# Sliding-window attention and a gated MLP in parallel: P times V of two pairs of head groups in one run

## Chip, cores and metric

The kernel runs on one core of a Trainium2 chip. The metric is the device time of one execution in microseconds, the median of several runs. The profile is one execution, taken by the hardware profiler; its times count from the first instruction.

## The reference

A layernorm without weights feeds two branches, which are added to the input: attention with 32 heads of 20 over a causal window of 256, and a gated MLP with a sigmoid gate. All inputs are bf16; x is 1 x 2048 x 640.

```python
xn = _layernorm(x)                                   # over D = 640
q, k, v = split_heads(xn @ wqkv)                     # 32 heads of 20
scores = (q @ k.T) * 20 ** -0.5                      # per head
mask = (i - j >= 0) & (i - j < 256)
o = softmax(where(mask, scores, -1e9)) @ v
A = o @ wo
B = (sigmoid(xn @ w_gate) * (xn @ w_up)) @ w_down    # F = 1536
return x + A + B
```

## The kernel before

The rows are worked on in four chunks `c` of 512. For each chunk there are these kinds of work for TensorE (PE):

- `qk`: ten projection blocks (`proj_block`, L297), five for Q and five for K, of five matmuls of 512 columns each. Q blocks are copied out of PSUM by VectorE (DVE, L301), K blocks by ScalarE (ACT, L303). The copies go by DMA into a DRAM scratch and come back in the layout that the scores need (`spread`, L315).
- `v`: eight half blocks (L326), two per 128 rows, five matmuls of 320 columns each; DVE copies out the first half, ACT the second.
- `gu`: twelve pairs of blocks `pg` and `pu` (L411, L418). ACT takes tanh of `pg`, DVE makes `h` from that and `pu` (L422).
- `out`: for each 128 rows the down projection (L432) and the attention output projection (L439) into the same two accumulators, then the residual (L443, DVE) and the store.
- scores: heads are in eight groups of four. Two groups, a pair `o` of 0, 2, 4 or 6, are worked on together, in four score steps in chunk 0 (`FIRST`) and five in the later ones (`LATER`). A step is 16 or 24 small matmuls (L487) on 20 x 64 tiles of the array, into one PSUM tile `ps` of four banks with one buffer. ACT takes the exponential of the whole tile into `pT` in SBUF (L493). Then the parts on the diagonal and on the window's old edge are masked: by GpSimd (POOL) with `affine_select` (L504), or, in the `late` steps, by DVE with a minimum against the tile `edge` (L497).
- P times V: `pv` (L520) multiplies all `pT` tiles of a pair with V, 72 matmuls in chunk 0 and 96 later, into two PSUM accumulators. `finish_group` turns each accumulator into `t1` with a DVE transpose (L532), and `scale_group` divides by the row sums and gathers the heads for the output projection (L540, L544, L548, all DVE).

All accumulators but `ps` come from the pool `ps_d` of four PSUM banks; each block needs one, a P times V two.

The order of work is written out by hand. The main loop (L719 on) goes over 76 score steps (16 in chunk 0, 20 in each later one). Around them an object `Fill` gives out the other PE work, the fill, from a list of labelled parts (L689 to L707). `fill.pull(ns)` takes blocks until their costs (1080 for a block, 680 for half a V block, and so on) add up to `ns`; `fill.until(label)` takes all up to that part. A part whose label is in `fill.shut` stops the pulling. After each score step at least `APART` = 1800 is pulled, and more by a credit, so that all the fill ahead of the next `out` part is spread over the steps up to a cut:

```python
credit += fill.left(label) / (last - t)
```

Work that is put off (`scale_group`) waits in `fill.behind`; each pulled block lets one of them go, or two where `hurry` is set. `due` says ahead of which step a pair's `pv` comes: one step after the pair's last score step, two in chunk 0. So before, the order is fill, `pv`, scores, fill, sixteen times less the last pair, which is worked on at the end.

Loads and stores are issued by SyncE (SP), in order; layernorm tiles are turned by DMA transposes on the same queue (`turn_block`, L283).

Of the kernel before, what the change touches and what calls it, by code (L numbers as in the profile page):

```python
# [9 lines left out]
P = 128  # L10
S = 2048
D = 640
# [3 lines left out]
DC = D // P  # L16
FC = F // P
CW = 512
NCH = S // CW
SBC = CW // P  # L20
HG = 4
NG = H // HG
GH = NG // 2
# [22 lines left out]
U = 64  # L46
PTW = 10 * U

# [14 lines left out]
FIRST = (  # L63
    dict(pieces=((0, 0, 5, 0), (5, 5, 3, 5)), diag=(0, 2), old=(4, 1), units=8),
    dict(pieces=((1, 1, 5, 0), (6, 6, 2, 5), (4, 7, 1, 7)), diag=(0, 2), old=(4, 1), units=8),
    dict(pieces=((2, 2, 5, 0), (7, 7, 1, 5)), diag=(0, 2), old=(4, 1), units=6),
    dict(pieces=((3, 3, 5, 0), (4, 4, 3, 5)), diag=(0, 2), old=(4, 1), units=8),
)
LATER = (
    dict(pieces=((2, 2, 5, 2), (-3, 0, 2, 0), (7, 7, 1, 7)), diag=(2, 2), old=(1, 2), units=8),  # L70
    dict(pieces=((3, 3, 5, 1), (6, 6, 2, 6), (-4, 0, 1, 0)), diag=(1, 2), old=(0, 2), units=8),
    dict(pieces=((0, 0, 5, 3), (-2, 0, 3, 0)), diag=(3, 1), old=(2, 2), units=8),
    dict(pieces=((1, 1, 5, 0), (5, 5, 3, 5)), diag=(0, 2), old=(4, 1), units=8),
    dict(pieces=((-1, 0, 4, 0), (4, 4, 4, 4)), late=3, units=8),
)
# [18 lines left out]
def kernel(  # L94
# [22 lines left out]
    xtp = pool("xtp", 2)  # L117
    stp = pool("stp", 6)
    qp = pool("qp", 3)
    kp = pool("kp", 5)  # L120
    vp = pool("vp", 10)
    hp = pool("hp", 15)
    pp = pool("pp", 5)
    op = pool("op", 7)
    onp = pool("onp", 2)
    tp = pool("tp", 2)
    np_ = pool("np", 2)
    ps_d = pool("ps_d", 4, space=bass.MemoryType.PSUM)
# [106 lines left out]

    edge = const.tile([P, HG, 2 * U], BF16, name="edge")

    def make_edge():
        nc.gpsimd.memset(edge, BIG)
        for k, base, sign in ((0, -1, -1), (1, 0, 1)):  # L240
            for a in range(2):
                view = edge[a * U:(a + 1) * U, :, k * U:(k + 1) * U]
                nc.gpsimd.affine_select(out=view, in_=view, pattern=[[0, HG], [sign, U]],
                                        compare_op=GE, fill=0.0, base=base, channel_multiplier=-sign)

    xnT = {}
    xns = {}

# [21 lines left out]
    def norm_block(c, s, mv, rstd):  # L270
        xn = lnp.tile([P, D], BF16, name="xn")
        nc.vector.tensor_scalar(out=xn, in0=xc[c][:, s, :], scalar1=mv[:, 0:1],  # L272
                                scalar2=rstd[:, 0:1], op0=SUB, op1=MULT)
        xns[c, s] = xn

    def transpose_rows(s, copy, lo=0, hi=DC):
        pt = ps_h.tile([P, DC, P], BF16, name="pt", tag="h")
        for d in range(lo, hi):
            nc.tensor.transpose(pt[:, d, :], xns[0, s][:, d * P:(d + 1) * P], ident)  # L279
        copy(out=xnT[0][:, lo:hi, s * P:(s + 1) * P], in_=pt[:, lo:hi, :])  # L280

    def turn_block(c, s):
        nc.sync.dma_start(out=xnT[c][:, :, s * P:(s + 1) * P], in_=xns.pop((c, s)), transpose=True)  # L283

# [81 lines left out]
    def g_qk(c):  # L366
        for w in "qk":
            for m in range(DC):
                proj_block(w, c, m)
                if c == 0 and w == "q" and m == 1:  # L370
                    load_x(1)
                if c == 0 and w == "q" and m == 3:
                    load_gu(wu, B_w_up, 0, FS // 2)
                if c == 1 and w == "q" and m == 3:
                    load_wo()
                if c and w == "k" and m == DC - 1:
                    spread("q", c, 0, GH)
                yield 5 * MM
        if c == 0:
            spread("q", c, 0, 2)  # L380
            spread("k", c, 0, 2)
            spread("q", c, 2, 4)
            spread("k", c, 2, 4)

    def g_v(c):
        for s in range(SBC):
            new_v(c, s)
            for hf in range(2):
                proj_v(c, s, hf, nc.scalar.copy if hf else nc.vector.tensor_copy)
                if hf == 0:  # L390
                    yield 5 * 136
            if s == 0:
                spread("k", c, 0, 2)
                spread("k", c, 2, GH)
            if s == 1:
                spread("q", c, GH, NG)
                spread("k", c, GH, NG)
            yield 5 * 136
# [81 lines left out]
    def scores(c, o, step):  # L480
# [12 lines left out]
        nc.scalar.activation(out=pt[:, :, 0:width], in_=ps[:, :, 0:width], func=EXP, scale=SCALE)  # L493
        if "late" in step:
            u = step["late"]
            view = pt[:, :, u * U:(u + 2) * U]
            return pt, lambda: nc.vector.tensor_tensor(out=view, in0=view, in1=edge, op=MIN)  # L497

        for (u, n), base, sign in ((step["diag"], 0, 1), (step["old"], -1, -1)):
            for a in range(2):  # L500
                two = pt[a * U:(a + 1) * U].rearrange("p h (a b) -> p h a b", a=2)
                k, b = divmod(u, SPAN)
                view = two[:, :, k:k + n, b * U:(b + 1) * U]
                nc.gpsimd.affine_select(out=view, in_=view, pattern=[[0, HG], [0, n], [sign, U]],  # L504
                                        compare_op=GE, fill=0.0, base=base, channel_multiplier=-sign)
        return pt, None

# [19 lines left out]

    on = {}

    def finish_group(c, g, acc):  # L530
        t1 = np_.tile([P, 16, 32], FP32, name="t1")
        nc.vector.transpose(out=t1.rearrange("p b r -> p (b r)"), in_=acc)  # L532
        if c < NCH - 1 or g < NG - 2:
            fill.behind.append(lambda: scale_group(c, g, t1))
        else:
            scale_group(c, g, t1)

    def scale_group(c, g, t1):
        rec = np_.tile([P, 16, 1], FP32, name="rec")
        nc.vector.reciprocal(rec, t1[:, :, DH:VW])  # L540
# [73 lines left out]
    def mean_act(s):  # L614
        xn = lnp.tile([P, D], BF16, name="xn")
        neg = lnp.tile([P, 1], FP32, name="neg")
# [8 lines left out]

    def norm_act(s, xn, neg, r):
        nc.vector.reciprocal(r, r)
        nc.vector.tensor_scalar(out=xn, in0=xc[0][:, s, :], scalar1=neg[:, 0:1],  # L628
                                scalar2=r[:, 0:1], op0=ADD, op1=MULT)
        xns[0, s] = xn  # L630

# [10 lines left out]
    for lo, hi in ((0, 3), (3, DC)):  # L642
        transpose_rows(0, act, lo, hi)
    norm_act(1, xn1, neg1, r1)
    mv3 = ln_mv(ln_half(0, 3, 1, stats3))
# [9 lines left out]
    v01 = project_v(0, 0, 1)  # L655
    norm_act(2, xn2, neg2, r2)
    copy_v(0, 0, 0, v00, act, (1,))
# [37 lines left out]
    fill.add("qk1", g_qk(1), 50 * MM)  # L695
    fill.add("v1", mix(g_v(1), g_gu(1, 0, 2), 1, 2), 40 * 136 + 2 * GU)
    fill.add("out0", mix(g_out(0, g_gu(1, 2, 3)), norms2, 1, 1), OUT + GU)
    fill.add("x3", later(load_x, 3), 0)
    fill.add("qk2", g_qk(2), 50 * MM)
    fill.add("v2", mix(g_v(2), g_gu(1, 3, 7), 0, 1), 40 * 136 + 4 * GU)  # L700
    fill.add("gu1b", mix(g_gu(1, 7, 12), norms3, 0, 1, False), 5 * GU)
    fill.add("out1", mix(g_out(1, g_gu(2, 0, 1)), itertools.chain(norms3, g_turns(3)), 1, 2), OUT + GU)
    fill.add("qk3", g_qk(3), 50 * MM)
    fill.add("v3", mix(g_v(3), g_gu(2, 1, 5), 0, 1), 40 * 136 + 4 * GU)
    fill.add("gu2", g_gu(2, 5, 12), 7 * GU)
    fill.add("out2", g_out(2, (), g_gu(3, 0, 1)), OUT + GU)
# [5 lines left out]

    due = {t + (1 if n else 2): (n, o) for (n, o), t in ends.items()}
    cuts = [(ends[n, NG - 2] + 2 + n, f"out{n}") for n in range(NCH - 1)] + [(len(todo), None)]
    fill.pull(6 * 5 * MM)
    parts = {}
    credit = 0
    fill.shut = {"out0", "out1", "out2"}
    for t, (c, k, o, step) in enumerate(todo):  # L719
        if k == 0 and c > 0:  # L720
            fill.until(f"qk{c}")
        if k == 2 and c > 0:
            fill.until(f"v{c}")
        if t in due:
            fill.flush()
            pair = due[t]
            fill.hurry = pair[1] == NG - 2
            pv(*pair, parts.pop(pair))
            if pair[1] == NG - 2:
                fill.shut.discard(f"out{pair[0]}")  # L730
        pt, late = scores(c, o, step)
        parts.setdefault((c, o), []).append((step, pt))
        last, label = next(x for x in cuts if t < x[0])
        credit += fill.left(label) / (last - t)
        rest = APART
        if late:
# [12 lines left out]

    homes = [("rows", 3)] * (SBC - 1) + [("xn", 4)]  # L750
    rows = [new_rows(c, s, *home, queue=nc.scalar) for s, home in enumerate(homes)]
    banks.close()
# [54 lines left out]
```

## Time and profile before

| | |
|---|---|
| time, median of 3 runs | 309.05 us (308.9 to 309.46) |
| profiled execution: span from first to last instruction | 307.5 us |
| the profiled execution's own time | not given beside its span; the median lies 1.55 us above the span |
| PE busy | 299.6 us, 97% |
| DVE, ACT, POOL busy | 170.7, 198.4, 169.3 us |
| scores (L487), P times V (L520) on PE | 1440 matmuls each; 8.7% and 6.0% of the chain of waits |
| `affine_select` on POOL (L504) | 256, 157.7 us |
| masks on DVE (L497) | 12, 5.1 us |
| granted TensorE clock | 1.000 |

Busy times are those of one engine; engines work beside each other. "Idle before" names what ended a wait. In the timeline a line gives the start, the time that the merged instructions took, the engine, the source line, and the tiles. The chain of waits follows the execution back from its last instruction, at each step to what released it.

### The profile page before, as it was taken

To read this page: it belongs to the slowest core of one execution; us is meant where nothing else is said; L and a number is where in the kernel's file an instruction comes from. 1 tells how busy PE (TensorE), PEld (TensorE's weight loads), DVE (VectorE), ACT (ScalarE), POOL (GpSimd) and SP (SyncE) were. 2 spreads that over 40 slices of the span, in tenths; PEclk is the share of its full clock that TensorE was granted. 3 is DMA by queue.
4 is the path that set the end of the run, shared out by engine and by line. 5 is a ranking of instruction groups with operands and counts; after the bars stand their busy time and mean duration, and the time that the engine had idled before them with its cause. 6 is when DMAs were issued, how large, how long until landed. Compare 5 with 4: busy or idle time off the path is not lost.

```text
span 307.5 us, 9944 instructions
## 1 busy us (share of the span) xinstructions
PE 299.6 (97%) x4276; PEld 167.5 (54%) x4311; DVE 170.7 (56%) x339; ACT 198.4 (65%) x197; POOL 169.3 (55%) x308
## 2 busy tenths in 40 slices
PE   7999999999999999999999999999999999999995
PEld 3654444555657654554457654554546664444774
DVE  5633666639698364487946164392824536363523
ACT  6933877698855649888674547878585547687000
POOL 6000686787874828576683729467372937566000
PEclk9999999999999999999999999999999999999999
DMA  7997976986407352820002712730000200000202
GB/s 215 366 344 236 324 158 214 337 238 209 154 2 139 58 179 68 272 83 2 3 3 67 129 58 87 250 122 0 5 0 2 87 26 21 2 2 7 83 21 67
DMA packets 40460, 35.68 MB, mean 116 GB/s; under 512 B 10560, under 2 KB 39872, under 8 KB 40384
## 3 DMA queue, kind: packets, MB, share of 16 engines
q1 hardware_dynamic: 39552, 34.27, 37.3%
q10 hardware_dynamic: 864, 0.77, 0.9%
q8 instruction: 34, 0.56, 0.8%
q14 instruction: 10, 0.08, 0.1%
HBM read 23.63 MB, written 10.26 MB: 110 GB/s over the span
## 4 chain that ended last, share of the span: by engine, by line
PE 96%; issue 1%; DMA 1%; DVE 1%; ACT 0%; SPq 0%
PE y L432 18%; PE pu L418 17%; PE pg L411 17%; PE pqk L297 14%; PE ps L487 9%; PE pv L326 7%; PE y L439 7%; PE acc L520 6%; DMA xc<-in_A_x_dram 1%; PE pt L279 0%; ACT xn L617 0%; DVE xn L272 0%; DVE xn L628 0%; SPq L156 0%; DVE stats L252 0%
## 5 line engine op out<-in xcount | busy, mean ns | idle before, releaser
L504 POOL TENSOR_SCALAR_AFFINE_SELECT pT<-pT 64x512 bf16<-64x512 bf16 (+1 forms) x256 | 157.7, 616 | 108.1 <-ACT pT L493 95.6
L493 ACT ACTIVATE pT<-ps 128x2048 bf16<-128x2048 f32 (+1 forms) x76 | 141.0, 1855 | 59.6 <-PE ps L487 54.6
L422 DVE SCALAR_TENSOR_TENSOR h<-th,pu 128x512 bf16<-128x512 f32 x48 | 32.8, 684 | 52.6 <-PE pu L418 46.1
L418 PE MATMUL pu<-xnT,wu 128*128 128x512 bf16 x228 | 59.0, 380 | 0.7 <-issue 0.2
L411 PE MATMUL pg<-xnT,wg 128*128 128x512 bf16 x226 | 58.5, 380 | 0.9 <-issue 0.3
L432 PE MATMUL y<-wd,h 128*128 128x320 bf16 (+2 forms) x396 | 56.7, 295 | 0.0
L432 PEld LDWEIGHTS <-h 128*128 128x128 bf16 x396 | 36.7, 98 | 15.8 <-issue 2.0
L414 ACT ACTIVATE th<-pg 128x512 f32<-128x512 f32 x48 | 28.6, 595 | 15.5 <-PE pg L411 15.4
L411 PEld LDWEIGHTS <-wg 128*128 128x128 bf16 x240 | 22.2, 98 | 25.8 <-issue 1.8
L418 PEld LDWEIGHTS <-wu 128*128 128x128 bf16 x240 | 22.0, 98 | 25.5 <-issue 2.0
L487 PE MATMUL ps<-qT,kT 20*64 20x320 bf16 (+4 forms) x1440 | 32.1, 260 | 0.0
L532 DVE STREAM_TRANSPOSE t<-acc 128x512 f32<-128x512 f32 x32 | 21.1, 697 | 19.7 <-PE acc L520 19.7
L487 PEld LDWEIGHTS <-kT 20*64 20x64 bf16 x1440 | 15.4, 103 | 24.9 <-issue 21.8
L443 DVE SCALAR_TENSOR_TENSOR rows<-y,rows 128x320 bf16<-128x320 f32 x30 | 14.4, 488 | 25.5 <-PE y L439 25.3
L544 DVE TENSOR_TENSOR on<-t,rec 128x320 bf16<-128x320 f32 (+4 forms) x48 | 27.8, 580 | 1.1
L326 PE MATMUL pv<-wv,xnT 128*128 128x320 bf16 x160 | 25.7, 300 | 0.0
L439 PE MATMUL y<-wo,oc 128*128 128x320 bf16 (+2 forms) x165 | 24.2, 295 | 0.0
L297 PE MATMUL pqk<-xnT,wk 128*128 128x512 bf16 x97 | 23.1, 381 | 0.2
L297 PE MATMUL pqk<-xnT,wq 128*128 128x512 bf16 x94 | 22.8, 381 | 0.4 <-issue 0.2
L335 DVE CAST v<-pv 64x320 bf16<-64x320 f32 x29 | 14.1, 486 | 12.5 <-PE pv L326 12.3
L520 PE MATMUL acc<-pT,v 64*32 64x320 bf16 (+4 forms) x1440 | 19.7, 253 | 0.0
L520 PEld LDWEIGHTS <-v 64*32 64x32 bf16 x1440 | 16.2, 91 | 5.8 <-ACT pT L493 1.7
(50 smaller groups left out, 178.7 us busy)
## 6 DMA issues: line engine op xcount, KB each, us to landing
qT<-sq SPq DMA_DIRECT2D x16, 256.0 KB
kT<-sk SPq DMA_DIRECT2D x16, 256.0 KB
sq<-st SPq DMA_DIRECT2D x20, 128.0 KB
sk<-st SPq DMA_DIRECT2D x20, 128.0 KB
out_dram<-rows SPq DMA_DIRECT2D x15, 160.0 KB
wg<-in_B_w_gate_dram SPq DMA_DIRECT2D x4, 480.0 KB
wu<-in_B_w_up_dram SPq DMA_DIRECT2D x4, 480.0 KB
xc<-in_A_x_dram SPq DMA_DIRECT2D x3, 640.0 KB
```

Of the source, the lines that this page charges most:

```text
L297: nc.tensor.matmul(ps, lhsT=wt[:, m, :], rhs=xnT[c][:, d, :], start=(d == 0), stop=(d == DC - 1))
L326: nc.tensor.matmul(ps[:, 0:HALF], lhsT=xnT[c][:, d, s * P:(s + 1) * P], rhs=wqkv[2][:, d, hf * HALF:(hf + 1) * HALF], start=(d == 0), stop ...
L411: nc.tensor.matmul(pg, lhsT=part(wg, d, f), rhs=xnT[c][:, d, :], start=(d == 0), stop=(d == DC - 1))
L414: nc.scalar.activation(out=th, in_=pg, func=TANH, scale=0.5)
L418: nc.tensor.matmul(pu, lhsT=part(wu, d, f), rhs=xnT[c][:, d, :], start=(d == 0), stop=(d == DC - 1))
L422: nc.vector.scalar_tensor_tensor(out=h, in0=th, scalar=1.0, in1=pu, op0=ADD, op1=MULT)
L432: nc.tensor.matmul(y[:, 0:cut[1] - cut[0]], lhsT=ht[c, f][:, s * P:(s + 1) * P], rhs=wd[:, f, cut[0]:cut[1]], start=(f == 0), stop=False)
L439: nc.tensor.matmul(y[:, 0:cut[1] - cut[0]], lhsT=oc[c, m][:, s * P:(s + 1) * P], rhs=wo[:, m, cut[0]:cut[1]], start=False, stop=(m == DC - 1))
L487: nc.tensor.matmul(ps[a * U:(a + 1) * U, i, col * U:(col + n) * U], lhsT=qk["k", kc, o // GH][32 * i:32 * i + DH, o % GH + a, kb * U:(kb + ...
L493: nc.scalar.activation(out=pt[:, :, 0:width], in_=ps[:, :, 0:width], func=EXP, scale=SCALE)
L504: nc.gpsimd.affine_select(out=view, in_=view, pattern=[[0, HG], [0, n], [sign, U]], compare_op=GE, fill=0.0, base=base, channel_multiplier ...
L520: nc.tensor.matmul(acc[32 * i:32 * i + 32, q * U:(q + n) * U], lhsT=vt[kb][a * U:(a + 1) * U, u, h * VW:h * VW + 32], rhs=pt[a * U:(a + 1) ...
```

## The change

P times V of two pairs now comes in one run, after the scores of its step instead of before, and no fill is pulled in that step. Chunks 0 to 2 have two such runs each, chunk 3 one, and then one single pair as before. To hold the probabilities of two pairs, `pT` has 11 buffers of 8 units (512) instead of 5 of 10. The pairs of masks in the step tables are split: two neighbouring units (an old edge and a diagonal) are masked by DVE in one minimum, in all steps of chunk 0 and three of five later; POOL masks the rest one unit at a time. `edge` holds one head's mask and is broadcast over four. There are fewer Q, K, V, `st` and `oc` tiles; the normalised rows are written in place, so the load of the next rows waits for their turning. V of each chunk is split into two parts; the second (`v1b`, `v2b`, `v3b`) is shut until the last P times V of the chunk before. The spreads of Q and K move from the projection parts into the main loop. With three `t1` tiles, the fourth accumulator of a run waits for the scaling of the first.

```diff
-PTW = 10 * U
+PTW = 8 * U
 FIRST = (
-    dict(pieces=((0, 0, 5, 0), (5, 5, 3, 5)), diag=(0, 2), old=(4, 1), units=8),
+    dict(pieces=((0, 0, 5, 0), (5, 5, 3, 5)), diag=(0,), pair=4, units=8),
...
 LATER = (
-    dict(pieces=((2, 2, 5, 2), (-3, 0, 2, 0), (7, 7, 1, 7)), diag=(2, 2), old=(1, 2), units=8),
-    dict(pieces=((3, 3, 5, 1), (6, 6, 2, 6), (-4, 0, 1, 0)), diag=(1, 2), old=(0, 2), units=8),
-    dict(pieces=((0, 0, 5, 3), (-2, 0, 3, 0)), diag=(3, 1), old=(2, 2), units=8),
-    dict(pieces=((1, 1, 5, 0), (5, 5, 3, 5)), diag=(0, 2), old=(4, 1), units=8),
-    dict(pieces=((-1, 0, 4, 0), (4, 4, 4, 4)), late=3, units=8),
+    dict(pieces=((2, 2, 5, 2), (-3, 0, 2, 0), (7, 7, 1, 7)), diag=(2,), old=(1,), pair=6, units=8),
+    dict(pieces=((3, 3, 5, 1), (6, 6, 2, 6), (-4, 0, 1, 0)), diag=(1,), old=(0,), pair=5, units=8),
+    dict(pieces=((0, 0, 5, 3), (-2, 0, 3, 0)), diag=(3,), old=(2, 7), units=8),
+    dict(pieces=((1, 1, 5, 0), (5, 5, 3, 5)), diag=(0, 5), old=(4,), units=8),
+    dict(pieces=((-1, 0, 4, 0), (4, 4, 4, 4)), pair=3, units=8),
 )
-    stp = pool("stp", 6)
-    qp = pool("qp", 3)
-    kp = pool("kp", 5)
-    vp = pool("vp", 10)
+    stp = pool("stp", 5)
+    qp = pool("qp", 2)
+    kp = pool("kp", 4)
+    vp = pool("vp", 8)
-    pp = pool("pp", 5)
-    op = pool("op", 7)
+    pp = pool("pp", 11)
+    op = pool("op", 6)
-    np_ = pool("np", 2)
+    np_ = pool("np", 3)
...
-        xn = lnp.tile([P, D], BF16, name="xn")
-        nc.vector.tensor_scalar(out=xn, in0=xc[c][:, s, :], scalar1=mv[:, 0:1],
+        xn = xc[c][:, s, :]
+        nc.vector.tensor_scalar(out=xn, in0=xn, scalar1=mv[:, 0:1],
...
     def finish_group(c, g, acc):
+        if len(turned) == 3:
+            fill.behind.pop(0)()
...
-    fill.add("v1", mix(g_v(1), g_gu(1, 0, 2), 1, 2), 40 * 136 + 2 * GU)
+    fill.add("v1", mix(g_v(1, 0, 2), g_gu(1, 0, 1), 1, 2), 20 * 136 + GU)
+    fill.add("v1b", mix(g_v(1, 2, 4), g_gu(1, 1, 2), 1, 2), 20 * 136 + GU)
...
-    fill.add("v2", mix(g_v(2), g_gu(1, 3, 7), 0, 1), 40 * 136 + 4 * GU)
-    fill.add("gu1b", mix(g_gu(1, 7, 12), norms3, 0, 1, False), 5 * GU)
+    fill.add("v2", mix(g_v(2, 0, 2), g_gu(1, 3, 5), 0, 1), 20 * 136 + 2 * GU)
+    fill.add("gu1b", mix(g_gu(1, 5, 12), norms3, 4, 1, False), 7 * GU)
+    fill.add("v2b", g_v(2, 2, 4), 20 * 136)
...
-    due = {t + (1 if n else 2): (n, o) for (n, o), t in ends.items()}
-    cuts = [(ends[n, NG - 2] + 2 + n, f"out{n}") for n in range(NCH - 1)] + [(len(todo), None)]
+    due = {}
+    for n in range(NCH):
+        wait = 1 if n else 2
+        for o in (0, 4):
+            if n == NCH - 1 and o == 4:
+                due[ends[n, o] + wait] = [(n, o)]
+            else:
+                due[ends[n, o + 2] + wait] = [(n, o), (n, o + 2)]
+    cuts = [(ends[n, NG - 2] + 3, f"out{n}") for n in range(NCH - 1)] + [(len(todo), None)]
-    fill.shut = {"out0", "out1", "out2"}
+    fill.shut = {"out0", "out1", "out2", "v1b", "v2b", "v3b"}
...
+    def products(pairs):
+        fill.flush()
+        if pairs[0][0]:
+            fill.until("v%db" % pairs[0][0])
+        last = pairs[-1][1] == NG - 2
+        fill.hurry = last
+        for pair in pairs:
+            pv(*pair, parts.pop(pair))
+        if last:
+            fill.shut -= {f"out{pairs[0][0]}", f"v{pairs[0][0] + 1}b"}
...
+        if k == 1 and c > 0:
+            spread("q", c, GH, NG)
+            spread("k", c, GH, NG)
+        if o >= GH and f"qk{c + 1}" in fill.done:
+            spread_first(c + 1)
+        pairs = due.get(t, ())
+        if len(pairs) == 1:
+            products(pairs)
         pt, late = scores(c, o, step)
         parts.setdefault((c, o), []).append((step, pt))
         last, label = next(x for x in cuts if t < x[0])
         credit += fill.left(label) / (last - t)
+        if len(pairs) == 2:
+            products(pairs)
+            if late:
+                late()
+            continue
```

`spread_first(c)` issues the first halves of Q and K of a chunk once, in two pieces each. The third chunk's V is split like the second's, with `gu2` ahead of `v3b`. The rows of the last chunk's residual are loaded into the tile of x instead of three `rows` tiles and one `xn`.

## Prediction

> **What bounds the kernel now.** I read the engine shares and the chain of waits first, then the timeline of PE, ACT and DVE around the P times V runs, then the groups by shape.
>
> ```profile
> PE 299.6 (97%) x4276; PEld 167.5 (54%) x4311; DVE 170.7 (56%) x339; ACT 198.4 (65%) x197; POOL 169.3 (55%) x308
> ...
> PE 96%; issue 1%; DMA 1%; DVE 1%; ACT 0%; SPq 0%
> ```
>
> TensorE is never kept waiting: 96% of the chain is its own work. A gain has to shorten its work, and any wait that a change gives it is added to the end. So the two questions are what PE time the change removes and whether PE ever waits.
>
> ```profile
> 28.01 1.24 PE L411 MATMUL pg<-xnT,wg 128*128 128x512 bf16 x5
> 29.09 1.24 PE L418 MATMUL pu<-xnT,wu 128*128 128x512 bf16 x5
> 30.26 0.42 PE L487 MATMUL ps<-qT,kT 20*64 20x320 bf16 x16
> ...
> 93.72 1.52 PE L439 MATMUL y<-wo,oc 128*128 128x320 bf16 x10
> 95.17 1.29 PE L520 MATMUL acc<-pT,v 64*32 64x320 bf16 x96
> 96.39 0.43 PE L487 MATMUL ps<-qT,kT 20*64 20x320 bf16 x24
> 96.75 2.62 PE L432 MATMUL y<-wd,h 128*128 128x320 bf16 x18
> ```
>
> Start to start: a fill block of five takes 1.08 (28.01 to 29.09), but 1.17 when a score step follows (29.09 to 30.26), so fill to small tiles costs 0.09. A P times V of 96 takes 1.22; it streams 40 units of 64 columns, 1.08 at the block's 1.08/2560 columns, so leaving it costs 0.14. A score step takes 0.36 and streams 512 columns, 0.22: another 0.14 to leave.
>
> ```profile
> 72.72 0.60 ACT L414 ACTIVATE th<-pg 128x512 f32<-128x512 f32 x1
> 73.22 1.44 ACT L493 ACTIVATE pT<-ps 128x1536 bf16<-128x1536 f32 x1
> 74.69 0.85 ACT L335 CAST v<-pv 64x320 bf16<-64x320 f32 x2
> 75.64 1.88 ACT L493 ACTIVATE pT<-ps 128x2048 bf16<-128x2048 f32 x1
> ```
>
> The score matmuls of the last line start at 75.06, so EXP starts 0.58 behind them and lasts 1.88. The score tile has one buffer: the next score step can't start sooner than 2.5 us after the last, however little lies between. Today two fill blocks (2.6 with the step) cover that.
>
> ```profile
> 146.66 1.31 DVE L532 STREAM_TRANSPOSE t<-acc 128x512 f32<-128x512 f32 x2
> 148.27 0.69 DVE L422 SCALAR_TENSOR_TENSOR h<-th,pu 128x512 bf16<-128x512 f32 x1 [0.30 <-PE pu L418]
> 148.88 0.25 DVE L540 RECIPROCAL rec<-t 128x16 f32<-128x16 f32 x1
> 149.16 0.75 DVE L544 TENSOR_TENSOR on<-t,rec 128x128 bf16<-128x128 f32 x1
> 149.94 0.71 DVE L548 STREAM_TRANSPOSE oc<-on 128x512 bf16<-128x512 bf16 x1
> 150.58 0.32 DVE L544 TENSOR_TENSOR on<-t,rec 128x192 bf16<-128x192 f32 x1
> 150.81 0.24 DVE L540 RECIPROCAL rec<-t 128x16 f32<-128x16 f32 x1
> 151.09 0.67 DVE L544 TENSOR_TENSOR on<-t,rec 128x320 bf16<-128x320 f32 x1
> 151.79 0.71 DVE L548 STREAM_TRANSPOSE oc<-on 128x512 bf16<-128x512 bf16 x1
> ```
>
> One P times V leaves DVE 1.3 of transposes and 3.55 (148.88 to 152.43) of scaling. It comes every fifth step, and DVE catches up between. These numbers price the merge.
>
> **The change, part by part.** *Merged runs.* Seven pairs are merged (two each in chunks 0, 1, 2, one in 3). Two separate runs pay fill to P 0.09, P to scores 0.14, scores to fill 0.14, twice: 0.74. Merged, the order is fill, S, P, P, S, fill: 0.09 + S to P + 0.14 + 0.14, with no switch between the P's. No row shows S to P; the nearest is scores to fill, 0.14, which I take: 0.23 saved, 7 x 0.23 = 1.6 us. With S to P at nothing it is 2.6, at twice 0.14 it is 0.6. [...]
>
> *The score steps around a merged run get no fill.* In chunks 1 to 3, S and two P take 0.36 + 1.08 + 1.22 = 2.66, over EXP's 2.5: nothing lost. In chunk 0 a P (72) takes 0.97, so 0.36 + 0.81 + 0.97 = 2.14: 0.4 lost at steps 9 and 17 each.
>
> *Fill runs dry at steps 15 to 17.* I walked the pacing by the kernel's own costs (1080 a block, 680 half a V block, at least 1800 per step). For the kernel before, the walk gives the trace's order of blocks. For the new one: `left("out0")` counts v1b (4880), but v1b stays shut until the merged run of step 17, so the open work is spent early. Step 14 gets pg, v, v; step 15 one block; step 16 none; step 17 the merged run. PE then waits on EXP. ACT is also late, with EXP and two copies per step (1.88 + 0.6 + 0.6 = 3.1, against 2.6 of PE) in steps 11 and 12 and 1.88 + 0.6 + 0.85 in step 13, so EXP of 15 starts 0.8 late. Step 14 waits 0.2, step 16 1.9 (S 0.36 and one block 1.08 in an interval of 3.3), step 17 2.15 (2.5 less 0.36), step 18 0.3: 4.5 us. Without the lag 3.8, with a longer one 5.
>
> *DVE after a merged run.* It now has four transposes (2.6), four groups to scale (7.0) and the masks, and each fill block that DVE empties queues behind them, with four PSUM banks in all. Step 36, from its score start: transposes at 1.7 to 3.65, scaling (2.2) to 5.85 because only three t1 fit, fourth transpose 6.5, mask 6.9, h of pu 7.6, two groups 10.6, mask 11.0, last group 12.7, h of the next pu 13.4, V copies (0.99 each) 14.4 and 15.4. PE from 3.0: three gate/up blocks to 6.2, V halves from 6.5; at 9.0 pu, v220 and v230 hold three banks for DVE, and the fourth passes two tiles through ACT; the second down tile waits for 13.4. PE ends these nine pieces at 15.1, where its work alone ends at 12.2: 3 us. Step 56 queues the same: 3 us. Step 17 has V at once and four layernorm blocks on DVE (1.0 each): PE reaches step 19 at 15.7, by its work 13.6: 2.1 us. Step 9 (Q copies on DVE) 0.5. Steps 26, 46 and 66 have ACT-emptied or gate/up blocks between: 0.3 together. Bounds: with DVE's products as short as its quickest rows (0.25 to 0.5, POOL quiet) 1, 1 and 0.7; if banks come round in strict turn, step 36 waits for h at 13.4 and for the V copies after it: 5.6 each.
>
> [...]
>
> *Masks.*
>
> ```profile
> L504 POOL TENSOR_SCALAR_AFFINE_SELECT pT<-pT 64x512 bf16<-64x512 bf16 x176 | 120.8, 686 | 101.8 <-ACT pT L493 93.9
> L504 POOL TENSOR_SCALAR_AFFINE_SELECT pT<-pT 64x256 bf16<-64x256 bf16 x80 | 37.0, 462 | 6.3 <-ACT pT L493 1.7
> L497 DVE TENSOR_TENSOR pT<-pT,edge 128x512 bf16<-128x512 bf16 x12 | 5.1, 425 | 8.0 <-ACT pT L493 7.9
> ```
>
> POOL goes from 256 selects to 272 narrow ones: 272 x 0.462 = 126 us for 157.7. DVE goes from 12 to 52 masks: 17 us more, and each waits for its EXP with the next evacuation behind it (7.9 over 7 waits, 1.1 each). With one block of two behind it and a bank to spare this is hidden; uncovered it is counted above.
>
> *SP and buffers, at nothing.* Spreads move from steps 12 to 15 (chunk 1) to steps 14 and 17. Queued ahead is the last K store; score step 16, 6 us on, waits for it. Cover: SP's waits for K stores are 2.1 over 5 in all. Uncovered: 1 us. load_x now waits for the turns, which are four steps older; behind it on SP are wo_i, wd and pads, due much later. Q, K, V, st and oc tiles fall free before their new use in the walk; the in-place norm has the same instruction.
>
> **Sum.** -1.6 + 0.4 (step 9) + 4.5 + 2.1 + 3 + 3 + 0.5 + 0.3 = +12.2 us, with 17's 0.3 in the 4.5. The profile gives a span of 307.5 and no other own time; the median 309.05 lies 1.55 above, taken as unchanged. Span 319.7, time 321.2.
>
> **The rivals.** *Banks cover the burst.* DVE's products run at their quick rows, and steps 36, 56, 17 give 1 + 1 + 0.7, the rest nothing: -1.6 + 0.4 + 4.5 + 2.7 = +6: 315. For: the trace has DVE four layernorm blocks behind at 87 to 91 with PE busy. Against: nine pieces, four banks.
>
> *The clock falls in the dry spell.* The granted clock is 1.00 in every window, the last included, where PE does 0.93 of 4.5 us; that speaks against it. The ten warm-up matmuls took 3.99 (0.40 each, later 0.216). If a spell sends PE back to that for 4 us, it costs 1.85; one to three spells: 323 to 327. [...]
>
> *Faster: the switch is worth more.* Place: the seven merged runs. All that a P times V pays beyond streaming is 0.09 + 0.14 + 0.14 = 0.37, so 2.6 at most. It decides only where all waits sum to less: it needs v1 to last through step 16 and the bursts hidden. Then 309.05 - 1.6 = 307.4. Against: the walk fits the trace.
>
> *The change does nothing*, both sides cancelling: needs 1.6 of waits, and step 16 alone has 1.9.
>
> **How the numbers follow.** Forecast 0.68 (316 to 326), covered burst 0.16, clock 0.11, faster 0.03, nothing 0.02. Time 321.2. Lower bounds (-2.6 + 0.4 + 3.8 + 2.7) give 313.4, upper ones (-0.6 + 0.8 + 5 + 3 + 5.6 + 5.6 + 1) 329.5; the range 313.4 to 327 leaves out the fast cases and the far end. Within 0.2% (0.6 us, what a measurement tells apart): 0.02; slower 0.95.
>
> **What would show it.** PE busy share of the span down to 93 to 94%; a PE gap of some 2 us before each of two neighbouring score steps ahead of the chunk 1 runs, released by ACT's pT; gaps before V or y released by DVE after the second merged run of chunks 1 and 2; P times V pairs of 2.3 start to start; POOL near 130 us, DVE near 188. Wrong if scores of step 16 have fill ahead, if PE stays at 97%, or if the gaps name a DMA.

## The result, and the profile after

The changed kernel takes 331.15 us (median of four, 328.71 to 336.62) beside 309.04 for the kernel before on the same chip: a ratio of 1.069, 95% interval 1.065 to 1.073. Runs over 1.5% above the fastest of their kernel are left out of the ratios: one of these four (336.62), and three of the four of x3_phase below. By the medians it is 22.1 us slower, where 12.2 was forecast, and 4 us above the range. The profiled execution has a span of 329.6; its own time, 331.34, is 1.7 above the span.

The engine shares, the clock row, the row of one DMA queue and the chain of the changed kernel:

```profile
PE 306.9 (93%) x4278; PEld 170.9 (52%) x4311; DVE 175.6 (53%) x379; ACT 198.9 (60%) x197; POOL 130.1 (39%) x324
...
PEclk9999999979799997999899999999999999999999
...
q8 instruction: 34, 0.56, 0.7%
...
PE 82%; DMA 6%; DVE 4%; issue 4%; ACT 3%; SPq 0%; ACTq 0%; DVEq 0%
```

PE's share is 93%, as forecast, but it gets there in two ways. Its idle time between instructions grew from 3.5 to 18.9 us, and its busy time from 299.6 to 306.9 although it does the same matmuls. The clock row tells why the second: it falls below 9 in four places. The trace has four stretches there, from 70.24, 83.89, 124.85 and 162.40, each 3.41 us long, at a granted clock of 0.50. In the chain there is now 4% of "issue", time in which PE waited for nothing that the profile shows.

The PE timeline at the dry spell of steps 16 and 17:

```profile
80.23 0.43 PE L479 MATMUL ps<-qT,kT 20*64 20x320 bf16 x24 [1.30 <-ACT pT L485]
82.76 0.43 PE L479 MATMUL ps<-qT,kT 20*64 20x320 bf16 x24 [2.10 <-ACT pT L485]
83.12 2.18 PE L510 MATMUL acc<-pT,v 64*32 64x320 bf16 x120
```

These are the two waits that were forecast, 1.30 and 2.10 for 1.9 and 2.15. Then the timeline behind the runs of steps 26 and 36, in the run of step 46, and at step 56:

```profile
119.28 2.39 PE L510 MATMUL acc<-pT,v 64*32 64x320 bf16 x192
121.60 0.33 PE L479 MATMUL ps<-qT,kT 20*64 20x320 bf16 x3
123.68 0.42 PE L479 MATMUL ps<-qT,kT 20*64 20x320 bf16 x21 [1.75 <-issue]
124.03 3.72 PE L297 MATMUL pqk<-xnT,wq 128*128 128x512 bf16 x9
...
161.75 0.42 PE L479 MATMUL ps<-qT,kT 20*64 20x320 bf16 x23 [2.73 <-issue]
...
200.39 1.54 PE L510 MATMUL acc<-pT,v 64*32 64x320 bf16 x113
203.47 1.10 PE L510 MATMUL acc<-pT,v 64*32 64x192 bf16 x79 [1.54 <-issue]
...
237.28 0.43 PE L479 MATMUL ps<-qT,kT 20*64 20x320 bf16 x24
237.64 2.41 PE L510 MATMUL acc<-pT,v 64*32 64x320 bf16 x192
239.98 0.43 PE L479 MATMUL ps<-qT,kT 20*64 20x320 bf16 x24
240.34 1.25 PE L410 MATMUL pu<-xnT,wu 128*128 128x512 bf16 x4
```

Step 56 shows the run as it was meant: two P times V in 2.34 (237.64 to 239.98), the whole run in 3.06. The others show what nobody ordered: PE stops in the middle of a score step, after 1 or 3 of its 24 matmuls, or in the middle of a P times V, for 1.5 to 2.7 us, with no releaser. In the trace, the matmul that ends each of these waits has no semaphore of its own to wait for. The line at 124.03 shows the half clock: nine recorded matmuls in 3.72, where the same nine take 2.35 at full clock (x4_split, below).

Counted in the order of PE's own instructions (weight loads and matmuls together), the five waits without a releaser end before numbers 3011, 4034, 5059, 6339 and 7363. Divided by 256 each leaves 194 or 195. Each comes with a transfer of 16 KB on the queue that the page calls `q8 instruction`, which starts 2.4 to 2.7 us before the wait ends; 16 KB for 256 instructions is 64 B each. The queue makes 34 such transfers, for 8704 instructions; PE has 4311 weight loads and as many matmuls, 8622, and some of its sequencer's. So I took PE to be waiting for its own code, which x3_phase below tests. A merged run and the two score steps at its sides are 2 x 48 + 2 x 192 = 480 PE instructions in 3.06 us; before, a score step and one P times V were 240, with fill on both sides. In the kernel before, two such places in the order are never passed less than 2.99 us apart, and there is no wait; in the changed kernel those with a wait are 3.2 us apart or more, the wait included. One pair was passed about 2.4 apart without a wait, at step 56, and the next place then had one of 0.72. So it is not a fixed limit for each single block.

One more new wait, from ACT's waits:

```profile
ACT st L303 <- DMA sq<-st: 9.4, 4, 5.3
```

ACT stands before K copies until an earlier store of Q has left its `st` tile (9.4 us in 4 waits), the EXP behind the copy is late, and PE loses 1.67 before the scores of step 13. Before, there was no such wait. The 6% of DMA in the chain is for the most part such a store: it was issued at 58.99 and took 5.21 us to land.

The gaps of PE sum up as: code 8.2 (1.75, 2.73, 1.54, 0.72, 1.42); steps 10, 16 and 17 waiting for EXP 3.7; step 13, and the first scores, which wait for a spread, 2.2; DVE's and ACT's evacuations 1.6. That is 15.6; the idle time in all grew by 15.4. The clock is the rest: four stretches lose up to 1.7 each, 6.8 of the 7.3 by which the busy time grew.

### The profile page after: what moved, and what is told of

Same layout as the page of the kernel before. It is cut to its first block, busy times and chain, and to the rows that moved or that the text cites. A ratio compares the mean times of both kernels' runs of the same rounds, so it can differ in the third digit from the quotient of the medians.

```text
span 329.6 us, 10023 instructions
## 1 busy us (share of the span) xinstructions
PE 306.9 (93%) x4278; PEld 170.9 (52%) x4311; DVE 175.6 (53%) x379; ACT 198.9 (60%) x197; POOL 130.1 (39%) x324
## 4 chain that ended last, share of the span: by engine, by line
PE 82%; DMA 6%; DVE 4%; issue 4%; ACT 3%; SPq 0%; ACTq 0%; DVEq 0%
PE y L424 16%; PE pg L403 15%; PE pu L410 14%; PE pqk L297 10%; PE ps L479 8%; PE y L431 7%; PE pv L326 6%; PE acc L510 5%; DMA sq<-st 4%; ACT pT L485 2%; DVE t L525 1%; DMA kT<-sk 1%; DMA xc<-in_A_x_dram 1%; DMA sk<-st 1%; DVE on L539 1%
## 5 line engine op out<-in xcount | busy, mean ns | idle before, releaser
L490 POOL TENSOR_SCALAR_AFFINE_SELECT pT<-pT 64x256 bf16<-64x256 bf16 x272 | 119.4, 439 | 165.0 <-ACT pT L485 152.8
L410 PE MATMUL pu<-xnT,wu 128*128 128x512 bf16 x227 | 60.0, 383 | 1.5 <-issue 0.9
L479 PE MATMUL ps<-qT,kT 20*64 20x320 bf16 (+4 forms) x1440 | 33.0, 261 | 10.3 <-ACT pT L485 5.3
L495 DVE TENSOR_TENSOR pT<-pT,edge 128x512 bf16<-128x512 bf16 x52 | 23.2, 447 | 32.5 <-ACT pT L485 31.5
L410 PEld LDWEIGHTS <-wu 128*128 128x128 bf16 x240 | 22.1, 98 | 27.3 <-issue 4.0
L435 DVE SCALAR_TENSOR_TENSOR rows<-y,rows 128x320 bf16<-128x320 f32 x24 | 11.5, 488 | 27.1 <-PE y L431 27.1
L297 PE MATMUL pqk<-xnT,wk 128*128 128x512 bf16 x98 | 24.4, 397 | 0.2
L297 PE MATMUL pqk<-xnT,wq 128*128 128x512 bf16 x95 | 24.2, 398 | 0.3
L326 PEld LDWEIGHTS <-xnT 128*128 128x128 bf16 x160 | 15.5, 100 | 10.3 <-issue 2.3
L303 ACT CAST st<-pqk 128x512 bf16<-128x512 f32 x20 | 11.2, 591 | 15.3 <-DMA sq<-st 9.4
```

The lines of the kernel that those rows point to most:

```text
L297: nc.tensor.matmul(ps, lhsT=wt[:, m, :], rhs=xnT[c][:, d, :], start=(d == 0), stop=(d == DC - 1))
L326: nc.tensor.matmul(ps[:, 0:HALF], lhsT=xnT[c][:, d, s * P:(s + 1) * P], rhs=wqkv[2][:, d, hf * HALF:(hf + 1) * HALF], start=(d == 0), stop ...
L410: nc.tensor.matmul(pu, lhsT=part(wu, d, f), rhs=xnT[c][:, d, :], start=(d == 0), stop=(d == DC - 1))
L479: nc.tensor.matmul(ps[a * U:(a + 1) * U, i, col * U:(col + n) * U], lhsT=qk["k", kc, o // GH][32 * i:32 * i + DH, o % GH + a, kb * U:(kb + ...
```

## Experiments

Theory A: the merged run is denser in instructions than their loading, and the waits and half clocks behind it are most of the loss. Rivals: the fill that runs dry, the fifth `st` tile, and DVE's bursts carry it, and the unnamed waits are one of these with its name missing.

**The V job of chunk 1 open, and six `st` tiles.** x1_open takes away the dry spell, x2_st6 the shortage of `st` tiles (paid for by one `oc` tile).

```
x1_open  - fill.shut = {"out0", "out1", "out2", "v1b", "v2b", "v3b"}
         + fill.shut = {"out0", "out1", "out2", "v2b", "v3b"}
x2_st6   - stp = pool("stp", 5);  op = pool("op", 6)
         + stp = pool("stp", 6);  op = pool("op", 5)
```

> The changed kernel with the second part of chunk 1's V (v1b) open from the start, so that fill is there at steps 15 to 17. If the dry spell is what costs there, the waits of PE on EXP of 1.30 and 2.10 us ahead of score steps 16 and 17 go, and the half-clock stretch of 3.4 us behind them (worth up to 1.7) with them: 331.2 becomes 326 to 328. One thing works against it: by the count of PE's instructions a block boundary then falls into the merged run of step 17, which under the code-loading theory below gives a new wait of about 1 us there. If instead the half clock comes from the merged runs themselves (small tiles counting as idle), it stays and only 3.4 us are won at most.

> The changed kernel with six st tiles again instead of five (and five oc tiles instead of six, to make the room). If the fewer st tiles are what keeps ACT's K copies of chunk 1 waiting for the stores of Q (9.4 us of such waits in the changed kernel, none before), the PE wait of 1.67 us ahead of score step 13 goes, the 0.5 us ahead of the first score step too, and the half clock from 70.2 us on: 331.2 becomes 327 to 329. If these waits come from the loads and pads ahead of the stores on SyncE whatever the number of tiles, nothing changes.

x1_open: 327.95 us (326.09 to 328.40), ratio 1.059 (1.054 to 1.064). The waits at steps 16 and 17 are gone (0.58 is left at step 18), and with them the half clock at 83.9; the waits for code stay at the same numbers: 3011, 4034, 5059, 6339, 7363. The wait of about 1 us that a new place in the run of step 17 might have brought did not come. Opening the V job is thus worth 3.2 us. x2_st6: 330.64 (329.80 to 333.94), ratio 1.071 (1.065 to 1.077), a miss. The wait before the first scores and the half clock at 70 went, but step 13 still waits 1.18 for EXP and step 16 now 2.61, for a spread of K, with half clocks of 6.83 at 80.6 and 162.5; one wait handed its time to the next.

**The same code at other places.** In x3_phase the ten warm-up matmuls of 512 columns at the start become 68 of 64, which shifts everything behind them by 116 PE instructions; apart from that, one PSUM tile of the pool is taken for the warm-up in place of two. x8_bphase does it to the kernel before, as its control.

```
- for n in (6, 4): ... nc.tensor.matmul(ps, lhsT=ones[:, 0:P], rhs=ones, ...)
+ for k in range(68): nc.tensor.matmul(ps[:, 0:U], lhsT=ones[:, 0:P], rhs=ones[:, 0:U], ...)
```

> The changed kernel with 68 short warm-up matmuls (64 columns) in place of 10 long ones: 116 more PE instructions ahead of all else, and no other change. In the changed kernel five PE waits of 1.0 to 2.95 us, for which the profile names no releaser, end at PE instruction 195 modulo 256, every one. Code loading (blocks of 256 instructions that a merged run of some 480 uses up faster than they come): the waits move with the blocks, ending again at 195 modulo 256 of the new count, that is 116 instructions earlier in the work; in runs of steps 26 and 36 inside the second P times V instead of the next score step; and with these places two boundaries fall into all seven runs instead of four or five, so 2 to 6 us slower than the changed kernel (333 to 337). VectorE, PSUM banks or the exponential: the waits stay where they are in the work, and the time is the same but for the start.

> The kernel before with the same 68 short warm-up matmuls (116 more PE instructions). Code loading: its longest stretch of small-tile instructions is 240, below a block of 256, so no shift of the blocks makes a wait: 309 to 310. If the slower time of the changed kernel with that warm-up came from the warm-up itself, it shows here too: 311 or more.

x8_bphase: 310.39 (308.81 to 310.99), a little above the 309 to 310 expected, ratio 1.001 (0.999 to 1.004): the shift alone costs at most 0.4%, and PE has no wait over 0.25 behind the first layernorm. x3_phase: 334.86 in its profiled execution, within the 333 to 337 expected; the median of all four is 339.95 (334.86 to 341.79). Two PE lines of that execution:

```profile
59.51 0.56 PE L509 MATMUL acc<-pT,v 64*32 64x192 bf16 x26 [2.78 <-issue]
...
124.96 0.82 PE L509 MATMUL acc<-pT,v 64*32 64x192 bf16 x55 [2.40 <-issue]
```

The waits moved back in the work (the one of step 26 from the scores behind the run into its second P times V, and a run of chunk 0 that had none now has 2.78), and they still end at 194 or 195 modulo 256 of the new count: 1218, 1986, 3011, 4034, 5315, 6339. Nothing was touched behind the warm-up, and the control has the same warm-up. This rules out that the waits are those of an operand with its name missing.

**Fill between the two P times V.** x4_split pulls two fill blocks between the products of a run and takes them off the credit; x9_busy adds 14 useless matmuls at steps 15 and 16 to that, to see what the half clock costs there.

```
x4_split  + pulled = 0
            for n, pair in enumerate(pairs):
          +     if n: pulled = APART - fill.pull(APART)
                pv(*pair, parts.pop(pair))
x9_busy   + if t in (15, 16): 5 or 9 matmuls of 512 columns into an unused bank
```

> The changed kernel with two fill blocks between the two P times V of a run (none at step 17, where no fill is open). Code loading: 256 instructions then last over 3 us everywhere, so the waits without releaser at steps 26, 36, 46, 56 and 66 (8 us in sum) go, and the half clock behind the first two (up to 3.4 us) with them; the run's saved tile switches (0.2 each) are lost again: 331.2 becomes 320 to 323. VectorE's burst after a run, as the prediction had it: the four transposes and the scaling come as before within a few us, so at most 3 us are won.

> The split version with 14 matmuls of no use (5 and 9, into a PSUM tile that nobody reads) in the two gaps of steps 15 and 16. Work and waits of the rest are as before; only PE is busy where it waited. If idleness of PE brings the half clock, its stretch of 6.8 us from 79.7 us on goes, and with it 3.4 us: 317.4 becomes 314. If the clock falls for another reason (small tiles, a load of current), nothing is won, or the extra blocks cost up to 1 us.

x4_split: 317.40 (316.71 to 320.28), ratio 1.028 (1.022 to 1.033), 13.75 us less than the changed kernel. It won more than expected. The step 26 run in its PE timeline:

```profile
118.25 0.43 PE L479 MATMUL ps<-qT,kT 20*64 20x320 bf16 x24
118.60 1.29 PE L510 MATMUL acc<-pT,v 64*32 64x320 bf16 x96
119.83 2.35 PE L297 MATMUL pqk<-xnT,wq 128*128 128x512 bf16 x9
122.11 1.29 PE L510 MATMUL acc<-pT,v 64*32 64x320 bf16 x96
123.33 0.43 PE L479 MATMUL ps<-qT,kT 20*64 20x320 bf16 x24
```

Nothing waits. All unnamed waits from step 26 to 66 are gone, and the DVE waits with them; what stays is the two waits at steps 16 and 17 (1.58, now for a spread of K, and 2.11 for EXP), step 13, and one half clock of 6.83 us at 79.7. x9_busy removed that half clock (granted clock 1.00 throughout) and took 317.34 (316.92 to 319.80): a miss, no gain. From the scores of step 16 to the first down projection it was 1.4 us quicker (12.23 to 10.84), and not 3.4, it seems because PE was waiting for EXP during much of the half clock; step 13 and two code waits (0.69 and 0.31, the count having moved) gave most of it back. So this half clock came with PE's idleness and went with it; that removing a stretch wins its full 1.7 only where PE has work is my estimate from these two runs.

**All three mended, and the merge alone undone.** x6_all is x1_open, x2_st6 and x4_split in one. x7_single keeps all of the change, with chunk 1's V job open, but does each P times V singly as before (`due` and `cuts` of before).

> Split runs, v1b open, six st tiles, together. If the three causes found so far (code loading in runs, fill shut at steps 15 to 17, the half clock behind both) are all there is, 317.4 of the split version loses its waits ahead of steps 16 and 17 (1.6 and 2.1) and its half-clock stretch of 6.8 us (3.4): 309 to 311, with some 1.5 us of waits left around step 13 and no half clock. If the masks on VectorE, the narrower tiles or VectorE's bursts cost something of their own, it stays at 313 or more.

> The changed kernel with every P times V by itself ahead of a score step, at the steps of the kernel before (and v1b open); masks, tile counts, the norm in place, the split V and the moved spreads stay as changed. If only the merging costs, 309 to 311, level with the kernel before but for the st tiles and the load of 52 masks on VectorE. If the masks or the smaller buffers cost by themselves, above 312.

x6_all: 313.64 (313.29 to 314.90), ratio 1.013 (1.011 to 1.016), above the 309 to 311 expected if nothing else cost: step 13 waits 1.18, step 16 waits 1.31 for a spread, and there is a new code wait of 1.78 behind the run of step 17, between whose products no fill was left to put. x7_single missed: 316.90 (315.80 to 318.95), ratio 1.024 (1.020 to 1.027), without any code wait. One wait, before step 12, does it, with 6.83 us of half clock that begin at 70.31, inside it. The PE timeline, SyncE's, and two pieces of the chain:

```profile
64.02 2.35 PE L297 MATMUL pqk<-xnT,wk 128*128 128x512 bf16 x9
71.21 0.66 PE L479 MATMUL ps<-qT,kT 20*64 20x320 bf16 x16 [4.83 <-ACT pT L485]
```

```profile
54.56 4.68 SPq L207 DMA_DIRECT2D wd<-in_B_w_down_dram  x5
...
61.45 4.19 SPq L305 DMA_DIRECT2D sq<-st  x4
65.69 2.92 SPq L219 DMA_DIRECT2D wo<-wo_i  x4
68.71 0.52 SPq L305 DMA_DIRECT2D sq<-st  x1
```

```profile
62.22 0.45 DVE st L301
62.67 6.30 DMA sq<-st
```

The stores that free the `st` tiles come behind weight loads (`wd`) on SyncE's queue. The one that ACT waits for was issued at 62.67, as soon as DVE's copy had ended, but it took 6.30 us to land; the DMA engines were 97%, 99% and 76% busy in the four-microsecond stretches from 56, 60 and 64. ACT waits 5.78 with the EXP of the next score step behind it. How much of the 6.30 is owed to the `wd` loads was not tried.

**The sixth `st` tile.** x10_single_st6 is x7_single with six `st` tiles and ten probability tiles; x11_before_st5 is the kernel before with five.

> As the kernel with every P times V single and the V job of chunk 1 not shut (316.9 us), but with six st tiles again, as before the change, and ten probability tiles in place of eleven, so that the memory suffices. Theory A: the sixth st tile is what the step 13 wait (4.83 us on TensorE before the scores, ACT waiting 5.78 us for the DMA sq<-st) and the half clock behind it come from: the wait shrinks below 1 us, the half clock at 70 us is gone, 309.5 to 311.5 us. Theory B: the st tile only gives the wait its name, and the order on SP's queue (the weight loads ahead of the sq stores) or the fewer K and Q tiles set it: a wait of 3 us or more stays before the step 13 scores under another releaser, 314 to 317 us.

> The kernel before with five st tiles in place of six, nothing else changed. Theory A: the one tile is enough to make ACT wait for sq<-st before a K copy near 65 us, TensorE then waits for pT before a score step, with the half clock possible behind it: 312 to 317 us. Theory B: the tile matters only together with what else the change moved (the single edge tile, the spreads now issued by step, the narrower probability tiles): no new wait over 0.5 us on TensorE, 309 to 310 us.

x10_single_st6: 310.34 (310.14 to 310.53), ratio 1.004 (1.003 to 1.005). The 4.83 before step 12 is gone and the half clock with it; 0.78 is left before step 13: 6.6 us for one `st` tile (and one probability tile fewer). x11_before_st5: 311.17 (310.30 to 313.32), ratio 1.008 (1.005 to 1.010), below the 312 that was expected, with this line on PE:

```profile
67.51 0.42 PE L487 MATMUL ps<-qT,kT 20*64 20x320 bf16 x16 [1.11 <-ACT pT L493]
```

So the tile alone makes that wait in the kernel before too, but 2 us of it; the rest needs the other edits. Which of them was not tried.

**The merge and nothing else.** x12_merge has the pools of x10_single_st6 and differs from it by the merged runs and their pacing (`due`, `cuts`) alone; x13_merge_split adds fill between their products.

> The changed kernel with six st tiles, ten probability tiles and the V job of chunk 1 not shut: it differs from the kernel of 310.34 us (same pools, each P times V single) by the merged runs alone. If the merged runs outrun the loading of TensorE's code: waits without a releaser of 0.8 to 4 us come back at the merged runs, each ending near place 195 of 256 in the order of TensorE's instructions, 6 to 9 us together, with one to three half-clock stretches of 3.4 us behind them; 318 to 325 us. If those waits came from the buffers (ACT or a DMA late, with the releaser's name missing in the trace): none of them is left with the sixth tile, and the merge brings its seven switches, 308.5 to 310 us.

> As the kernel with merged runs, six st and ten probability tiles, V of chunk 1 not shut, but with two fill blocks between the two P times V of a run, so that no stretch of small tiles holds 480 instructions; the switches saved are given back. If the loading of the code is the price of the merge and nothing else: no wait over 0.5 us is left at steps 26 to 66, 310 to 312 us, at most 2 us above the single form (310.34 us). If the two P times V at one place cost by themselves too (TensorE's fill used up at steps 15 to 18, DVE's bursts): 313 us or more, with waits there.

x10_single_st6, x12_merge and x13_merge_split, one line each of their engine shares:

```profile
PE 302.9 (98%) x4311; PEld 168.0 (54%) x4311; DVE 177.0 (57%) x379; ACT 198.6 (64%) x197; POOL 131.6 (43%) x324
```

```profile
PE 306.3 (94%) x4311; PEld 169.6 (52%) x4311; DVE 176.3 (54%) x379; ACT 198.8 (61%) x197; POOL 131.3 (40%) x324
```

```profile
PE 302.9 (97%) x4311; PEld 168.2 (54%) x4311; DVE 175.7 (56%) x379; ACT 198.9 (64%) x197; POOL 131.2 (42%) x324
```

x12_merge: 328.10 (326.04 to 329.36), ratio 1.059 (1.055 to 1.062), 3 us above its range. Against 310.34 the merge costs 17.8 us; in the spans (326.4 and 308.5) 17.9, of which 14.6 is gaps and 3.4 busy time, two half-clock stretches at 1.7. Its PE timeline at steps 27 and 37:

```profile
117.43 0.38 PE L479 MATMUL ps<-qT,kT 20*64 20x320 bf16 x12 [0.49 <-ACT pT L485]
120.46 0.28 PE L479 MATMUL ps<-qT,kT 20*64 20x128 bf16 x12 [2.65 <-issue]
...
155.74 1.85 PE L510 MATMUL acc<-pT,v 64*32 64x320 bf16 x144
160.27 0.43 PE L479 MATMUL ps<-qT,kT 20*64 20x320 bf16 x24 [2.68 <-issue]
```

Six waits end at 193 to 195 modulo 256 (1985, 3011, 4034, 5059, 6339, 7363), 1.28 + 2.65 + 2.68 + 0.89 + 0.54 + 1.73 = 9.8 us; the trace gives the last of them a releaser (POOL), but its place in the order is the same. With the 3.4 of the clock, whose two stretches begin within 0.7 us of the end of such a wait, that is 13.2 of the 17.8.

x13_merge_split: 313.76 (312.76 to 316.74), ratio 1.016 (1.012 to 1.020): 14.3 us less than x12_merge, which bears out the 13.2. It is 3.4 above the single form, more than the 2 expected of the code alone; its profiled run has 1.44 at step 13, 0.98 at step 16 and one code wait of 0.66. I put that down to two P times V at one place; it was not taken apart further.

The three runs divide the loss: 1.2 (before to x10_single_st6, net: narrower tiles, masks on VectorE, spreads, fewer Q, K and V tiles) + 14.3 (code and the clock behind it) + 3.4 (two P times V at one place) + 3.1 (x12_merge to the changed kernel: the fifth `st` tile and the shut V job) = 22.0. The steps lead from one kernel to the other, so that they add up says nothing by itself; what each is worth is shown only in that order. Single edits don't add up, as x2_st6 shows, since waits cover each other.

No version here beats the kernel before. The merge saves its switch only while the small tiles follow each other without fill, and there the loading of the code falls behind.

## Why the prediction was right or wrong

**The switch: right.** Step 56 takes 3.06 for S, P, P, S. By the prediction's own terms two separate runs take 0.74 of switches and 2 x (1.08 + 0.22) of streaming, 3.34; the merged one 3.06 and 0.09 to enter: 0.19 saved for the 0.23 taken. Seven such runs would give 1.3 for 1.6; the one at step 56 is measured.

**"In chunks 1 to 3, S and two P take 2.66, over EXP's 2.5: nothing lost": this step failed.** It set PE's work against EXP alone. The run asks for 480 instructions in 3.06 us; where it waited, 256 took 3.2 us or more, the wait included. It lost 8.2 in waits, and two of the half clocks (124.85, 162.40) begin within 1.2 us of such a wait's end, 3.4 more. Neither forecast nor rivals held this wait. The trace of before held its resource, the `q8 instruction` queue, and I had not asked how quickly PE runs through its code.

What passing such a place in the order cost is measured: no wait without a releaser over 0.2 us in the kernel before, 0.72 to 2.73 us in the changed kernel's five, up to 3.9 in x3_phase.

**The clock: wrong.** It was a rival at 0.11, of one to three spells at 1.85; there were four of at most 1.7. What spoke against it in the prediction, full clock after 0.93 of 4.5 us of work, was a window at the end of the span; in that same trace the clock falls to 0.50 at 308.03, half a microsecond behind the span. In x7_single it fell 3.9 us into a wait and stayed down for 6.83 us. In the changed kernel it fell with far less idleness, behind waits of 1.67 (before step 13), 1.75 and 2.73, for 3.41 us each time.

The length of the wait alone does not decide it: no half clock follows the 1.69 before step 13 in x9_busy, whose granted clock is 1.00 throughout. In the changed kernel's trace the stretches begin a whole number of times 3.41 us apart; the four, at 70.24, 83.89, 124.85 and 162.40, are 4, 12 and 11 times that apart. In the 3.41 us ahead of each, PE was busy for 1.66, 1.31, 1.60 and 0.68 us. Of the other pieces of 3.41 us on the same grid, from 12 us on, only the one at the span's end has less than 1.99: it has 0.42, and 0.50 is granted again from its end, 329.65, on. That PE's busy time in the piece ahead decides is my reading of this one trace; no run was made to test it.

**The dry spell: right in kind.** 3.4 at steps 16 and 17 and 0.26 at step 10, for 4.5 and 0.4. Its half clock at 83.89 was not in the sum. The spreads, put at nothing, have no wait here but 0.51 at the first scores; in x2_st6, x4_split, x6_all and x12_merge, though, the wait before step 16 ends with a spread of K (2.61, 1.58, 1.31 and 1.31), which is the uncovered case.

**The bursts of DVE: over-sized.** 2.1 + 3 + 3 + 0.5 + 0.3 = 8.9 was forecast. In the changed kernel 1.6 is put down to evacuations, 1.3 of it after step 56:

```profile
243.08 0.59 DVE L495 TENSOR_TENSOR pT<-pT,edge 128x512 bf16<-128x512 bf16 x1
243.59 0.68 DVE L414 SCALAR_TENSOR_TENSOR h<-th,pu 128x512 bf16<-128x512 f32 x1
...
246.96 0.49 DVE L539 TENSOR_TENSOR on<-t,rec 128x320 bf16<-128x320 f32 x1
247.49 0.71 DVE L543 STREAM_TRANSPOSE oc<-on 128x512 bf16<-128x512 bf16 x1
248.13 0.65 DVE L414 SCALAR_TENSOR_TENSOR h<-th,pu 128x512 bf16<-128x512 f32 x1
```

The queue is the forecast one: mask, h of the first pu, groups, mask, the last group, h of the next pu; PE waited 1.05 for that last h. The size failed for two reasons. The products are at their quick rows (0.49 for the 128x320, where 0.67 stood in the lines taken), as the "covered burst" rival had it: DVE is busy 175.6, not 188. And the code waits gave DVE time to catch up; how much is not measured, but x13_merge_split, without those waits, has no wait of PE on DVE over 0.2 either behind the first layernorm, its bursts being apart. (One scaling, by the rows that the prediction shows, ends at 152.50 and takes 3.62, not 3.55; that is too little to matter.)

**Masks: right.**

```profile
L490 POOL TENSOR_SCALAR_AFFINE_SELECT pT<-pT 64x256 bf16<-64x256 bf16 x272 | 119.4, 439 | 165.0 <-ACT pT L485 152.8
L495 DVE TENSOR_TENSOR pT<-pT,edge 128x512 bf16<-128x512 bf16 x52 | 23.2, 447 | 32.5 <-ACT pT L485 31.5
```

119.4 for 126, 23.2 for 5.1 + 17; POOL 130.1 in all. x10_single_st6 has all these masks and is 1.2 us from the kernel before.

**"Q, K, V, st and oc tiles fall free before their new use": wrong for st alone.** I walked the copies by engine time and not by when the store that frees the tile has landed, 5.21 us after its issue here and 6.30 in x7_single. It costs 1.67 and a half clock here, 6.6 us in the single form. The Q, K and V pools and the probability tiles are within the 1.2 us of x10_single_st6.

## What to carry to other kernels

Before small-tile runs are put together, count the engine's instructions, not only its time: here runs of 480 in 3.06 us stopped in the middle of their work, where 256 took 3.2 us or more with the wait, and two ordinary blocks in between took away all such waits from step 26 on (x4_split). A wait with no releaser that recurred at the same place modulo 256 of the engine's order was its code here; shifting that order by some harmless instructions is a cheap test. A tile that a store empties came free here when the store had landed, 5.21 us after its issue and 6.30 in x7_single, so a buffer is to be counted with that time, read from the trace.

## What the runs showed of the hardware

- PE passed 288 instructions in 1.85 us (144 matmuls of a P times V and their weight loads, 6.4 ns each), and then stood for 2.68 (x12_merge, run of step 36); in the changed kernel, two neighbouring places at 195 modulo 256 were 3.2 us apart or more wherever it waited.
- The changed kernel's five waits for code ended 2.4 to 2.7 us after the start of a 16 KB transfer on the `q8 instruction` queue.
- The granted clock of the changed kernel fell to 0.50 four times inside the span, for 3.41 us each, at whole multiples of 3.41 us from one another; PE had been busy for 1.66, 1.31, 1.60 and 0.68 us of the 3.41 us before.
- A store of 128 KB issued while the DMA engines were 99% busy took 6.30 us to land (x7_single).
